# Two attention blocks in one kernel: four score banks per head group on VectorE, processed in pairs, and PV grouped by head

## Chip, cores and metric

The kernel runs on one core of one Trainium2 chip. The metric is the device time of one execution in microseconds. Of the kernel before there are eight runs, with a median of 482.88 us.

## What is computed

The input of each of two attention blocks, A and B, is 2048 rows of 448 bf16 numbers; their outputs stand side by side in rows of 896. Both have 16 heads of 28.

```python
# A: 16 query heads share one key head and one value head
q = (x @ wq).reshape(B, S, H, Dh).transpose(0, 2, 1, 3)
k = x @ wk
v = x @ wv
scores = einsum("bhqd,bkd->bhqk", q, k) * Dh ** -0.5
o = einsum("bhqk,bkd->bhqd", softmax(scores), v)
a = o.transpose(0, 2, 1, 3).reshape(B, S, H * Dh) @ wo
# B: each position sees 8 keys of its own head, at distances 0, 2, ..., 14
logits = einsum("bhsd,bhswd->bhsw", q, kg) * Dh ** -0.5   # masked where the index is negative
b = einsum("bhsw,bhswd->bhsd", softmax(logits), vg).transpose(0, 2, 1, 3).reshape(B, S, D) @ wo
```

A needs 16 x 2048 x 2048 exponentials. They are most of ScalarE's work.

## The kernel before

**The order of the work.** The program is planned in Python before it is built. Every instruction, or small group of them, is added to a list with its engine, an estimated duration, the tiles that it reads (R) and writes (W), a priority `pr` (lower goes first) and sometimes an earliest time. `Sched.run` then plays a list scheduler: whenever an engine is free, it takes the ready operation of lowest priority number. The resulting order on each engine is fixed in the program, and each engine waits on semaphores where the plan has a dependency. Score matmuls and exponentials of A have priority -50, the first VectorE pass -45, PV -40, the later VectorE passes -0.5, the evictions of B -1; other work has its due time in microseconds.

**Part A.** The queries are taken in 4 stretches of 512 rows (`sc`), the 16 heads in 4 groups of four (`t`), so there are 16 head groups ("quads") in time. In each, a unit is one head `j` against one block `tb` of 128 keys: a score bank of 128 keys by 512 queries in PSUM. There are 16 x 4 = 64 units in a quad and 1024 in all. They are taken in order, head innermost, three and two at a time in turn, into two sets of score banks (banks 0 to 2, and 3 and 4), numbered `n`. For each set (`a_loop`):

- PE makes the scores, either with 32 rows of the array (line 740) or, where the planner wants a denser PE, with 128 rows against a zero-padded key copy (line 738);
- ScalarE takes the exponential of the set in one instruction (line 756) into one of the 7 slots of the ring `expT`;
- PE multiplies four units at a time with the values and sums (`v_aug`, line 770) into bank 5; the four matmuls of a group are for the heads j = 0 to 3 of one key block, each in its own 32 columns of the array.

Some units are not given to ScalarE. `offload` takes the last bank of every third three-bank set (`n` a multiple of 6, 28 to 396, key blocks 1 to 13), 51 in all. `d_exp` computes their exponential on VectorE in five passes over 512 columns: a scaled conversion of the score bank to int32 (line 802, the only one that reads PSUM, so it frees the bank), the exponent bits (line 805), two products with the fraction bits (lines 807 and 809), and their product in bf16 into `dexp` (line 812). The result has a constant factor, which a second set of values in `v_aug` takes out. A PV group that has such a unit reads three slices of `expT` and one of `dexp`.

At the end of a quad VectorE copies bank 5 out (line 825), and the sums, their reciprocals (line 836), the copies on GpSimd (line 838) and the final projection (line 861) follow.

**Part B** runs beside A in 16 blocks of 128 positions, with due times 25 us apart: projections (lines 902 and 918), products of queries and shifted keys on VectorE (line 943), sums on PE (line 952), maximum and difference on VectorE (lines 964 and 966), for two blocks together an exponential on ScalarE (line 977), its sum (line 979), reciprocal (line 981) and normalised factors (line 983), then products with the shifted values (line 996), additions (line 1000), transposing matmuls that also sum (line 1007) and the projection (line 1014).

**Filler.** A planner rule adds matmuls on zeros, whose results are not used, where PE would otherwise have little to do (lines 357, 380 and 735).

**Shared memory.** In the first microseconds the tile `d_i` holds the query weights, which GpSimd and VectorE copy out at line 574, and `d_u` holds the squares of the keys (lines 621 and 627, read at line 629).

## Time and profile before

| | |
|---|---|
| median of 8 runs | 482.88 us (482.83 to 488.87) |
| profiled execution: its time, its span | 482.85 us, 480.9 us |
| busy: PE, VectorE, ScalarE, GpSimd | 452.5, 378.9, 456.9, 40.8 us |
| granted TensorE clock | 1.0 |
| first exponential of A starts, last ends | 12.73, 471.85 us |
| idle of ScalarE before exponentials of A | 8.7 us |

In the profile PE is TensorE's matmuls, PEld its weight loads, DVE VectorE, ACT ScalarE, POOL GpSimd and SP SyncE; L756 is line 756 of the kernel. A group of instructions is given as line, engine, operation, output<-inputs, partitions x elements of both with their types, and the count; then busy time in us, the mean duration in ns, and the engine's idle time just before these instructions with what released it. The mean duration counts the overlap of one instruction with the next, so it can exceed the time from start to start. The 40 slices give each engine's busy share in tenths. The chain is followed back from the last instruction to what released it.

### The profile page before, as it was taken

The numbers are of one execution on the slowest core, as the hardware profiler recorded it, in microseconds if no ns is written. First come the engines' busy times: TensorE is split into PE (matmuls) and PEld (weight loads), VectorE is DVE, ScalarE is ACT, GpSimd is POOL, SyncE is SP. The second block draws the span as 40 slices with busy tenths as digits, with TensorE's granted clock in tenths as the row PEclk, the third lists the DMA queues.
The fourth block names the chain that finished last, engine by engine and source line by source line (L and its number), as shares of the span: only waits on it lengthen the run. The fifth ranks groups of instructions, "written<-read, shape, count | busy, mean of one in ns | idle before, by whom it ended". The sixth has DMA issues, their size and how long they took to land.

```text
span 480.9 us, 8734 instructions
## 1 busy us (share of the span) xinstructions
PE 452.5 (94%) x3630; PEld 177.0 (37%) x3630; DVE 378.9 (79%) x703; ACT 456.9 (95%) x431; POOL 40.8 (8%) x71
## 2 busy tenths in 40 slices
PE   8999999999999999999999999998999999998886
PEld 3433334333343443333343433333344243333333
DVE  3335887998778888888878888888968989888673
ACT  3999999999999999999999998999999999999993
POOL 8742000000000000000000000000000000000000
PEclk9999999999999999999999999999999999999999
DMA  8790201020200220002020330002200320202001
GB/s 162 150 228 13 88 27 60 11 78 13 85 11 30 97 95 12 11 2 86 11 93 4 116 97 11 10 11 79 95 12 1 115 99 17 67 24 96 0 1 57
DMA packets 42071, 27.34 MB, mean 57 GB/s; under 512 B 17090, under 2 KB 41968, under 8 KB 42032
## 3 DMA queue, kind: packets, MB, share of 16 engines
q1 hardware_dynamic: 40080, 25.65, 18.5%
q10 hardware_dynamic: 1776, 0.81, 0.7%
q8 instruction: 28, 0.46, 0.4%
q0 software_dynamic: 176, 0.33, 0.3%
q14 instruction: 11, 0.09, 0.1%
HBM read 17.60 MB, written 5.52 MB: 48 GB/s over the span
## 4 chain that ended last, share of the span: by engine, by line
ACT 63%; PE 34%; DMA 1%; DVE 1%; ACTq 0%; issue 0%; DVEq 0%
ACT expT L756 62%; PE ps L740 7%; PE ps L902 6%; PE ps L770 5%; PE ps L738 4%; PE ps L688 2%; PE ps L918 2%; PE ps L830 1%; PE ps L1014 1%; DMA d_i<-in_A_wq_dram 1%; PE ps L615 1%; PE ps L861 1%; PE ps L1007 1%; PE ps L651 1%; PE ps L702 0%; PE ps L380 0%
## 5 line engine op out<-in xcount | busy, mean ns | idle before, releaser
L756 ACT ACTIVATE expT<-ps 128x1024 bf16<-128x1024 f32 (+1 forms) x410 | 449.7, 1222 | 8.7 <-PE ps L740 3.3
L740 PE MATMUL ps<-qT,kT 32*128 32x512 bf16 x734 | 110.2, 384 | 12.4 <-ACT expT L756 9.7
L770 PE MATMUL ps<-expT,v_aug 128*32 128x512 bf16 x973 | 97.6, 389 | 0.1
L738 PE MATMUL ps<-qT,kz 128*128 128x512 bf16 x290 | 84.1, 382 | 8.8 <-ACT expT L756 6.9
L740 PEld LDWEIGHTS ps<-qT,kT 32*128 32x128 bf16 x734 | 27.1, 91 | 81.3 <-ACT expT L756 58.6
L943 DVE TENSOR_TENSOR stage<-qTB,kTB 112x1024 bf16<-112x1024 bf16 x64 | 44.1, 707 | 4.0 <-PE ps L952 4.0
L770 PEld LDWEIGHTS ps<-expT,v_aug 128*32 128x32 bf16 x973 | 24.1, 93 | 62.7 <-issue 57.9
L802 DVE TENSOR_SCALAR d_i<-ps 128x512 int32<-128x512 f32 x51 | 35.3, 693 | 14.3 <-PE ps L740 13.1
L838 POOL COPY rrep<-rden 128x512 bf16<-128x512 bf16 x15 | 12.7, 846 | 399.4 <-DVE rden L836 399.4
L902 PE MATMUL ps<-xT_B,wqkv 128*112 128x512 bf16 (+1 forms) x128 | 43.2, 405 | 0.2 <-DVE qT L711 0.2
L996 DVE TENSOR_TENSOR prod<-Vsh,a_n 128x896 bf16<-128x896 bf16 x64 | 38.2, 627 | 0.0
L807 DVE SCALAR_TENSOR_TENSOR d_u<-d_i 128x512 f32<-128x512 uint16 x51 | 36.1, 707 | 0.0
L809 DVE SCALAR_TENSOR_TENSOR d_v<-d_i,d_e 128x512 f32<-128x512 uint16 x51 | 35.3, 692 | 0.0
L812 DVE SCALAR_TENSOR_TENSOR dexp<-d_u,d_v 128x512 bf16<-128x512 f32 x51 | 34.9, 684 | 0.0
L738 PEld LDWEIGHTS ps<-qT,kz 128*128 128x128 bf16 x290 | 19.3, 99 | 35.0 <-ACT expT L756 28.3
L952 PEld LDWEIGHTS ps<-ones,stage 112*128 112x128 bf16 x512 | 20.9, 96 | 13.4 <-issue 7.9
L952 PE MATMUL ps<-ones,stage 112*128 112x4 bf16 x512 | 25.2, 167 | 0.2 <-DVE qT L711 0.2
L1007 PE MATMUL ps<-ident,padd 128*112 128x128 bf16 x256 | 25.1, 226 | 0.0
L1007 PEld LDWEIGHTS ps<-ident,padd 128*112 128x112 bf16 x256 | 18.9, 129 | 12.3 <-issue 9.4
L902 PEld LDWEIGHTS ps<-xT_B,wqkv 128*112 128x112 bf16 (+1 forms) x128 | 14.3, 127 | 22.1 <-issue 17.2
L805 DVE TENSOR_SCALAR d_e<-d_i 128x512 int16<-128x512 int16 x51 | 21.6, 424 | 0.2
L830 PEld LDWEIGHTS ps<-sel,PV_sb 128*128 128x128 f32 x128 | 18.9, 190 | 5.5 <-issue 3.9
(109 smaller groups left out, 439.7 us busy)
## 6 DMA issues: line engine op xcount, KB each, us to landing
Vsh<-v_scratch SPq DMA_DIRECT2D x16, 896.0 KB, 4.7
v_scratch<-Vst SPq DMA_DIRECT2D x16, 112.0 KB, 1.7
out_dram<-outB SPq DMA_DIRECT2D x16, 112.0 KB, 1.7
out_dram<-outA SPq DMA_DIRECT2D x14, 112.0 KB, 1.8
wqkv<-in_B_wqkv_dram SPq DMA_DIRECT2D x1, 672.0 KB, 4.8
stage<-in_A_x_dram ACTq DMA_DIRECT2D x1, 448.0 KB, 3.7
wo_B<-in_B_wo_dram SPq DMA_DIRECT2D x4, 98.0 KB
wo<-in_A_wo_dram SPq DMA_DIRECT2D x4, 98.0 KB
```

The lines of the kernel that those rows point to most:

```text
L738: r = e.matmul(g.bank(b0 + i), g.kz[:, j, 128 * tb:128 * tb + 128], g.qT[:, sc % 2, t, :], start=True, stop=True)
L740: r = e.matmul(g.bank(b0 + i), g.kT[32 * j:32 * j + 32, 128 * tb:128 * tb + 128], g.qT[32 * j:32 * j + 32, sc % 2, t, :], start=True, stop ...
L756: x = a("act", t_exp(w), lambda e, b0=b0, w=w, n=n: e.activation(g.expT[:, n % ERING, 0:w], g.ps[:, 512 * b0:512 * b0 + w], ACT.Exp, scale ...
L770: x = e.matmul(g.bank(PVBANK, p0=32 * j, p1=32 * j + 32), g.v_aug[:, w, tb, :], src, start=tb == 0, stop=tb == 15, tile_position=(0, 32 * j))
L802: a("dve", t_dve_ps(512), lambda e: e.tensor_scalar(out=ii, in0=g.bank(bank), scalar1=A2 * F, scalar2=-127 * F, op0=ALU.mult, op1=ALU.max) ...
L807: a("dve", t_dve_1x(512), lambda e: e.scalar_tensor_tensor(out=uu, in0=lo, scalar=EP * F, in1=lo, op0=ALU.add, op1=ALU.mult), R=[("d_i", h ...
L809: a("dve", t_dve_1x(512), lambda e: e.scalar_tensor_tensor(out=vv, in0=lo, scalar=ER * F, in1=ee.bitcast(BF16), op0=ALU.add, op1=ALU.mult) ...
L902: a("pe", t_mm(512), lambda e, u=u, t=t, kt=kt, w=w: e.matmul(g.bank(u.bank, p1=KC), g.wqkv[64 * (kt // 3):, kt, w * D + KC * t:w * D + KC ...
L943: op = a("dve", t_dve_2x(1024), lambda e, t=t, qv=qv, kv=kv: e.tensor_tensor(out=g.prodT[0:KC, t, :, :], in0=qv, in1=kv, op=ALU.mult), R=R ...
L952: r = e.matmul(g.bank(u.bank, 128).rearrange("p (h w) -> p h w", w=WIN)[:, 4 * t:4 * t + 4, w], g.prodT[0:KC, t, w, :], g.ones4[:, :], sta ...
L996: a("dve", t_dve_2x(2 * D), lambda e, qr=qr, Vv=Vv, av=av: e.tensor_tensor(out=g.prod2[:, 2 * qr:2 * qr + 2, :].rearrange("p w (d h) -> p ...
L1007: a("pe", 0.09, lambda e, u=u, t=t, w=w: e.matmul(g.bank(u.bank, 128, 128 * t, p1=KC), g.padd[:, w, KC * t:KC * t + KC], g.ident[:, :], st ...
```

## The change

Four units of each quad but the last go to VectorE, one for each head. They are the last banks of the three-bank sets 0, 2, 5 and 7 of the quad, counting only three-bank sets that lie in it whole; in the first quad sets 4, 6, 7 and 9. That is 60 units. The first pass (line 802) still takes one bank when it comes, but into one half of a 1024-column tile; the four other passes are done once for two units, over 1024 columns. One of the two middle results now overwrites `d_i`.

PV groups are formed by head: as units of ScalarE arrive, each waits in a list of its head, and whenever all four heads have one, the first of each make a group, whatever their key blocks. The four units of VectorE make a group of their own. A quad still has 16 groups; the first in the order of forming starts the sums and the last ends them.

In part B the exponential of line 977 writes its result with the window index ahead of the head index, so that its writes are 64 bytes apart, and the factors of line 983 are read and written in that same order. `padd` is no longer a tile of its own but the first half of `prod2`. The value projections of A in `a_v` may get a filler matmul (352 columns) ahead of the first matmul of each block.

```diff
-OFF_EVERY, OFF_FROM, OFF_TO = 6, 28, 396
-DR = 4
+OFF_AT = {q: (0, 2, 5, 7) for q in range(1, 15)}
+OFF_AT[0] = (4, 6, 7, 9)
+DR = 2
...
-                if o.use is not None and o.use.spare and area(T) < self.WANT:
+                if o.use is not None and o.use.spare and o.alone and area(T) < self.WANT:
...
-        self.dexp = sb([128, DR, 512], BF16, "dexp")
-        self.d_i = sb([128, 2, 512], mybir.dt.int32, "d_i")
-        self.d_e = sb([128, 2, 512], mybir.dt.int16, "d_e")
-        self.d_u = sb([128, 1, 512], FP32, "d_u")
-        self.d_v = sb([128, 1, 512], FP32, "d_v")
+        self.dexp = sb([128, DR, 1024], BF16, "dexp")
+        self.d_i = sb([128, 2, 1024], mybir.dt.int32, "d_i")
+        self.d_e = sb([128, 1024], mybir.dt.int16, "d_e")
+        self.d_u = sb([128, 1024], FP32, "d_u")
...
-        self.padd = sb([128, 4, D], BF16, "padd")
+        self.padd = self.prod2[:, 0:4, :]
...
-        u = Use(f"V{c}", g.LB)
+        u = Use(f"V{c}", g.LB, spare=160)
...
+                o.alone = kt == 0
...
+        quads = {(sc, t): [[] for _ in range(4)] for sc in range(4) for t in range(4)}
+        dunits = []
...
-                where.append((us[i], ("expT", n % ERING), g.expT[:, n % ERING, 512 * i:512 * i + 512], 0))
+                quads[us[i][:2]][us[i][3]].append((us[i], ("expT", n % ERING), g.expT[:, n % ERING, 512 * i:512 * i + 512]))
...
-                where.append((us[na],) + g.d_exp(b0 + na, slot) + (1,))
-            while len(where) >= 4 or (where and pos == NU):
-                grp, where = where[:4], where[4:]
-                sc, t, tb, _ = grp[0][0]
-
-                def pv(e, grp=grp):
-                    for (sc, t, tb, j), _, src, w in grp:
-                        x = e.matmul(g.bank(PVBANK, p0=32 * j, p1=32 * j + 32), g.v_aug[:, w, tb, :], src,
-                                     start=tb == 0, stop=tb == 15, tile_position=(0, 32 * j))
-                    return x
-                o = a("pe", 0.33, pv, R=sorted({y[1] for y in grp}) + [(k, w, tb // 4) for k in ("v_aug", "v_aug1") for w in sorted({y[3] for y in grp})],
-                      W=["pv"] if tb in (0, 15) else [], pr=-40, dense=700)
-                if tb == 0:
-                    quad = [o]
-                elif tb < 15:
-                    o.deps.add(quad[0])
-                    quad.append(o)
-                else:
-                    o.deps.update(quad)
-                if pv_first:
-                    o.claims = [PVBANK]
-                    pv_first = False
-                if tb == 15:
-                    g.a_quad_end(sc, t)
+                dunits.append((us[na],) + g.d_exp(b0 + na, slot))
+                if len(dunits) == 4:
+                    g.pv_group(dunits, 1)
+                    dunits = []
+            for u in us:
+                js = quads[u[:2]]
+                while all(js):
+                    g.pv_group([x.pop(0) for x in js], 0)
+
+    def pv_group(self, grp, w):
+        g, a = self, self.s.add
+        qd = grp[0][0][:2]
+        n = len(g.pvs.setdefault(qd, []))
+        first, last = n == 0, n == 15
+
+        def pv(e):
+            for (_, _, tb, j), _, src in grp:
+                x = e.matmul(g.bank(PVBANK, p0=32 * j, p1=32 * j + 32), g.v_aug[:, w, tb, :], src,
+                             start=first, stop=last, tile_position=(0, 32 * j))
+            return x
+        o = a("pe", 0.33, pv, R=sorted({y[1] for y in grp}) + sorted(
+            {(k, w, y[0][2] // 4) for k in ("v_aug", "v_aug1") for y in grp}), W=["pv"] if first or last else [], pr=-40, dense=700)
+        if len(g.pvs) == 1 and first:
+            o.claims = [PVBANK]
...
+        g.pvs[qd].append(o)
+        if last:
+            g.a_quad_end(*qd)
...
-        return int(n % OFF_EVERY == 0 and OFF_FROM <= n <= OFF_TO and 0 < us[-1][2] < 14)
+        g = self
+        if n % 2 or us[0][:2] != us[-1][:2]:
+            return 0
+        if us[0][:2] != g.quad:
+            g.quad, g.round = us[0][:2], n // 2
+        return int(n // 2 - g.round in OFF_AT.get(4 * us[0][0] + us[0][1], ()))
...
+            a("dve", 0.68, lambda e: e.tensor_scalar(out=ee, in0=hi, scalar1=127.0, scalar2=128.0, op0=ALU.add, op1=ALU.mult),
+              R=di, W=["d_e"], pr=-0.5)
+            a("dve", t_dve_1x(1024), lambda e: e.scalar_tensor_tensor(
+                out=uu, in0=lo, scalar=EP * F, in1=lo, op0=ALU.add, op1=ALU.mult), R=di, W=["d_u"], pr=-0.5)
+            a("dve", t_dve_1x(1024), lambda e: e.scalar_tensor_tensor(
+                out=ii.bitcast(FP32), in0=lo, scalar=ER * F, in1=ee.bitcast(BF16), op0=ALU.add, op1=ALU.mult),
+              R=["d_e"], W=di, pr=-0.5)
+            a("dve", t_dve_1x(1024), lambda e: e.scalar_tensor_tensor(
+                out=out, in0=uu, scalar=EQ * F * F, in1=ii.bitcast(FP32), op0=ALU.add, op1=ALU.mult),
+              R=["d_u"] + di, W=[("dexp", m % DR)], pr=-0.5)
+        return ("dexp", m % DR), out[:, 512 * h:512 * h + 512]
...
+        ew = g.e_t[:, par].rearrange("p b w h -> p b h w")
...
-        a("act", t_act(256), lambda e: e.activation(fl(g.e_t), fl(g.lg2), ACT.Exp, scale=SCALE),
+        a("act", t_act(256), lambda e: e.activation(ew, g.lg2[:, par], ACT.Exp, scale=SCALE),
...
-            a("dve", 0.62, lambda e, b=b: e.tensor_tensor(
-                out=g.a_n[:, par, b].rearrange("p w h -> p h w"), in0=g.e_t[:, par, b],
-                in1=g.rs[:, b, :].unsqueeze(2).to_broadcast([128, H, WIN]), op=ALU.mult),
+            a("dve", 0.32, lambda e, b=b: e.tensor_tensor(
+                out=g.a_n[:, par, b], in0=g.e_t[:, par, b],
+                in1=g.rs[:, b, :].unsqueeze(1).to_broadcast([128, WIN, H]), op=ALU.mult),
...
-              R=[("prod2", hf), ("prod2", hf + 2)], W=[("padd", hf)], pr=pr)
+              R=[("prod2", hf), ("prod2", hf + 2)], W=[("padd", hf), ("prod2", hf)], pr=pr)
```

## The prediction, made before the changed kernel was run

> **What bounds the kernel now.** I read the summary page first, then the groups of instructions by shape, the waits of ScalarE, the table of stages and the timeline around ScalarE's longest pauses. The page's busy shares, 40 slices and chain of waits:
>
> ```profile
> span 480.9 us, 8734 instructions
> ...
> PE 452.5 (94%) x3630; PEld 177.0 (37%) x3630; DVE 378.9 (79%) x703; ACT 456.9 (95%) x431; POOL 40.8 (8%) x71
> ...
> DVE  3335887998778888888878888888968989888673
> ACT  3999999999999999999999998999999999999993
> ...
> PEclk9999999999999999999999999999999999999999
> ...
> ACT 63%; PE 34%; DMA 1%; DVE 1%; ACTq 0%; issue 0%; DVEq 0%
> ACT expT L756 62%; PE ps L740 7%; PE ps L902 6%; PE ps L770 5%; PE ps L738 4%; PE ps L688 2%; PE ps L918 2%; PE ps L830 1%; PE ps L1014 1%; DMA d_i<-in_A_wq_dram 1%; PE ps L615 1%; PE ps L861 1%; PE ps L1007 1%; PE ps L651 1%; PE ps L702 0%; PE ps L380 0%
> ```
>
> ScalarE is busy in nine tenths or more of every slice between head and tail, and the chain that ends last lies on it for 63%, nearly all of that in the exponential of line 756. VectorE stands at 79%, near nine tenths in many slices but only at three in the first 36 us. The granted TensorE clock is full throughout. PE's 94% includes filler matmuls and modelled ends. So the end is set by ScalarE's stream: it starts at 12.73 us, its last exponential ends at 471.85, and 9.05 us of tail follow to 480.9. The profiled execution took 482.85 us, 1.95 more than its span, and the median of the runs is 482.88; I count from 482.85.
>
> The groups by shape (count, then busy us and mean ns, then idle before and its releaser):
>
> ```profile
> L756 ACT ACTIVATE expT<-ps 128x1024 bf16<-128x1024 f32 x255 | 258.6, 1064 | 4.6 <-PE ps L770 3.2 <-PE ps L740 0.8 <-PE ps L738 0.2
> L756 ACT ACTIVATE expT<-ps 128x1536 bf16<-128x1536 f32 x154 | 229.0, 1487 | 4.0 <-PE ps L740 2.5 <-PE ps L738 0.9
> ...
> L807 DVE SCALAR_TENSOR_TENSOR d_u<-d_i 128x512 f32<-128x512 uint16 x51 | 36.1, 707 | 0.0
> L802 DVE TENSOR_SCALAR d_i<-ps 128x512 int32<-128x512 f32 x51 | 35.3, 693 | 14.3 <-PE ps L740 13.1 <-PE ps L738 0.7
> ...
> L805 DVE TENSOR_SCALAR d_e<-d_i 128x512 int16<-128x512 int16 x51 | 21.6, 424 | 0.2
> ...
> L983 DVE TENSOR_TENSOR a_n<-e_t,rs 128x128 bf16<-128x128 f32 x16 | 11.4, 755 | 0.1
> ...
> L849 DVE TENSOR_TENSOR oTn<-PV_sb,ps 128x512 bf16<-128x512 f32 x15 | 10.5, 697 | 1.3 <-PE ps L844 1.1
> ...
> L966 DVE TENSOR_TENSOR lg<-ps,mx 128x128 f32<-128x128 f32 x15 | 4.3, 284 | 0.0
> ...
> L977 ACT ACTIVATE e_t<-lg 128x256 f32<-128x256 f32 x8 | 3.6, 455 | 0.0
> ...
> L579 POOL COPY wvB<-Vsh 128x448 bf16<-128x448 bf16 x3 | 2.9, 977 | 0.3
> ...
> L574 POOL COPY wq<-d_i 128x448 bf16<-128x448 bf16 x3 | 1.7, 561 | 0.2
> ```
>
> Two numbers carry the forecast. An exponential over three banks takes 1487 ns and one over two 1064: a bank costs ScalarE 423 ns. And ScalarE stood idle before exponentials for only 8.7 us in all, 3.2 of it in three pauses that a PV matmul (line 770) ended, the ring of expT having no free slot. The timeline of one of them (start, length, engine, line):
>
> ```profile
> 115.62 6.54 ACT L756 ACTIVATE expT<-ps 128x1024 bf16<-128x1024 f32 x6
> ...
> 121.00 0.68 DVE L812 SCALAR_TENSOR_TENSOR dexp<-d_u,d_v 128x512 bf16<-128x512 f32 x1
> ...
> 122.76 0.39 PE L770 MATMUL ps<-dexp,v_aug 128*32 128x512 bf16 x1
> ...
> 123.20 1.94 ACT L756 ACTIVATE expT<-ps 128x1024 bf16<-128x1024 f32 x2 [1.03 <-PE ps L770]
> ```
>
> ScalarE pauses 1.03 us until the PV group at 122.76 has read its inputs. In that group is a dexp operand, which VectorE finished only at 121.68. The pause of 0.5 us near 184 ends on such a group too; the longest, 1.6 us near 289, ends on a group with no dexp in it.
>
> **The change, part by part.** *Banks moved.* Followed through the numbering of score sets, the new rule takes four banks in each of 15 head groups, 60 against 51 now. So 9 three-bank exponentials become two-bank ones, and the number of exponentials stays: 9 x 0.423 = 3.8 us off the binding stream.
>
> *What such a shortened set costs its neighbours.* From starts in the trace, the floor from one exponential to the next is 0.904 us for two banks and 1.331 for three; a shortened set lies 0.064 us above its floor on average, a full one 0.020. Nine more: 9 x 0.044 = 0.4 us back.
>
> *PV regrouped.* No ScalarE group waits for VectorE any more, so the two pauses that end on dexp groups should go: 1.0 + 0.5, and with the overlap of consecutive exponentials lost at a pause (about 0.2 each), 1.9 us. The third I keep, as its group was all ScalarE's: there PE's written order put a score matmul, itself waiting for ScalarE, ahead of the PV that ScalarE needed. Grouping by head makes some units wait for the next key block, four units or 1.6 of the 7 ring slots, less than the chain of five VectorE passes that the ring holds out now. The bounds are a gain of 3.7 (all three go) and a loss of the same size (the delayed heads fill the ring as often); I take 1.9.
>
> *VectorE's passes.* A bank now costs 693 + 424 + 707 + 692 + 684 = 3200 ns, 163.2 us for 51. Between lines 966 (128 columns, 284 ns) and 849 (512, 697) a column costs 1.076 ns, so a pass over 1024 takes about 1.25 us, and the integer pass 424 + 0.26 (half a column's price each, as its 424 suggests) = 0.69 us. A pair: 2 x 0.693 + 0.69 + 3 x 1.25 = 5.83 us, 30 pairs 174.8: 11.6 us more. Line 983 writes its 16 x 8 factors one bf16 every 32 bytes and takes 755 ns, where line 966 with as many columns takes 284; written in order, 16 x 0.47 = 7.5 us go. The sum of line 979 now reads with a stride, at most another 2 us. VectorE goes from 378.9 to some 385 us, still 81%: it costs nothing itself, as long as the three-bank set is freed in time. That is the cover to watch: in all 51 cases of the trace VectorE begins line 802 at a median of 0.05 us after the set's last score matmul and is done 0.70 us (median) before the next score matmul into that set, which again ends 0.18 before its exponential. So a read may be late by 0.88 us for nothing. A pass of 0.69 begun just before never breaks that; one of 1.25 does by up to 0.37. VectorE would be inside such a pass for 90 x 1.25 = 112 of 481 us, 23%: 60 x 0.23 = 14 reads meet one, in three of ten the rest is over 0.88, mean excess 0.18: 0.7 us as PE sees it, of which I take half, 0.35, since VectorE often stands waiting for PE there (13.1 us before line 802). Bounds: nothing, and 60 x 0.37 = 22.
>
> *Softmax factors of part B.* Line 977, on ScalarE, now writes its 256 float32 values 64 bytes apart, where it wrote in order for 455 ns. No ScalarE row shows such a write. Lower bound: no cost. Upper bound: the price of line 983, (755 - 284)/128 = 3.7 ns for each element, so 0.94 us for each of 8, 7.5 us, all on the binding stream. Between them lies GpSimd's pair: line 579 copies 448 columns that it gathers 56 bytes apart in 977 ns, line 574 as many in order in 561: 0.93 ns for each element, 256 x 0.93 = 0.24 us, 1.9 in all. I take that one: another engine than VectorE, and no two-byte writes to merge, although it is a read.
>
> The Trainium skill speaks against this edit: "SBUF — State Buffer", in its note on 16-byte lines, says that every access that crosses to a new line pays a penalty. The 755 against 284 ns of VectorE's strided write agree; whether ScalarE pays is shown by no run here. It gives no size, so the sum stays as it is.
>
> *Rest, taken at nothing.* padd written over the first half of prod2 makes line 996 of the next block wait for the transposes (line 1007) of this one; before, line 1000 had that wait one step later, and it cost 0.7 us once, on VectorE. Should it grow, part B ends later, but its last add starts at 466.8 and its transposes wait in PE's order until 474, so some 5 us cover it. Up to 16 filler matmuls among the v projections in the first 35 us (320 ns each where line 380 does it, up to 16 x 0.3 = 4.8 us of PE) run at the lowest priority; ScalarE idles only 1.1 us in that stage, and their cost is between nothing and perhaps 2 us. The first banks now go to VectorE near 22 us, when the weights that share d_i have been copied out (GpSimd ends line 574 at 12.2) and VectorE is 42% busy (13.2 of 31.6 us). The tail has no offloaded bank and stays.
>
> Sum: 482.85 - 3.8 + 0.4 - 1.9 + 0.35 + 1.9 = **479.8 us**, 0.6% below. About 0.5%, 2.4 us, is what a measurement of this kernel can tell from no change, so this stands just beyond it.
>
> **The rivals.** *A, everything hidden:* ScalarE's strided write is free and all three pauses go: 479.8 - 1.9 - 1.8 = 476.1. For it: line 977 is a plain activation whose output rate nothing here shows to be the limit. Against: pauses come from a written order, and a new order has its own.
>
> *B, the pauses move:* the head that lacks a bank holds its three partners in the ring, and what VectorE held ScalarE for, the ring does: 479.8 + 1.9 = 481.7. For it: a third of the idle time before exponentials is already the ring's.
>
> *C, slower than before: the strided write on ScalarE.* At line 983's price it is 7.5 instead of 1.9 us: 485.4. It decides from the point where the other terms, 5.0 us, are eaten: 5.0/8 = 0.62 us more for each line 977, 1.08 in place of 0.455 us. For it: same geometry, same memory. Against: four bytes instead of two in each write.
>
> *D, VectorE frees the banks late:* if 20 of 60 reads meet a full pass, 20 x 0.37 = 7.4: 486.8. For it: stages of 25 us busy in 28. Against: the read has priority among what is ready, and the median slack of 0.70.
>
> That the change does less than it says can be left out: the count of 60 follows from its numbering.
>
> **How the numbers follow.** The forecast (478 to 481.5) 0.42, A 0.13, B 0.17, C 0.16, D 0.12. Below 480.4: most of the forecast (0.33), A, a little of B, together 0.50. Above 485.3: half of C and D, 0.20. Between: 0.30. The range: A's 476.1 with 0.6 for hidden late reads below, 475.5; above, C and the nearer part of D, 486.0. Forecast's own range: 478 to 481.5.
>
> **What would show it.** The shapes of line 756: 145 with 1536 columns in place of 154, and the same mean durations. Line 977's mean: 455 (A), about 0.7 us (forecast), 1.08 and more (C). Pauses of ScalarE ended by line 770: one, of none on dexp. Line 802 ending as a releaser of score matmuls: D. Line 983 near 0.28 us and the 1024-column passes near 1.25. I am wrong if the mean of line 756 itself moves, if pauses before it grow past 12 us, or if the clock row falls below full anywhere.

## The result

The changed kernel takes 484.44 us (median of 21 runs), the kernel before 482.76 (median of 62 runs). The ratio is 1.0029, with an interval of 1.0014 to 1.0045: 0.3% slower, where 479.8 us, 0.6% faster, had been forecast. The profiled execution took 483.81 us, 0.96 more than that of before, and I compare these two. All medians and ratios of the experiments are of their fast runs, and of two, `to_q15` and `q_prio`, the one profile is of a slow run, with the clock at half for 34 and 41 us.

The summary page of the changed kernel: span, busy shares, the 40 slices of VectorE, ScalarE and the granted clock, the chain of waits by engine:

```profile
span 481.9 us, 8626 instructions
...
PE 453.6 (94%) x3612; PEld 178.9 (37%) x3612; DVE 391.6 (81%) x628; ACT 455.1 (94%) x431; POOL 47.0 (10%) x71
...
DVE  3478887898898888988898898997898899698373
...
ACT  3995999999999999999999999999999999999994
...
PEclk9998999999999999999999999999999999999999
...
ACT 61%; PE 32%; DVE 2%; POOL 2%; DMA 1%; issue 1%; ACTq 0%; DVEq 0%; POOLq 0%
```

ScalarE's stream is unbroken except in one slice: the fourth, 36 to 48 us, shows 5 tenths, and in the same slice the clock falls to 8 tenths. GpSimd, absent from the chain of before, now holds 2% of it. The groups by shape:

```profile
L760 ACT ACTIVATE expT<-ps 128x1024 bf16<-128x1024 f32 x264 | 264.9, 1051 | 7.0 <-PE ps L742 5.7 <-PE ps L744 1.1
L760 ACT ACTIVATE expT<-ps 128x1536 bf16<-128x1536 f32 x145 | 214.0, 1476 | 4.8 <-PE ps L744 4.0 <-PE ps L742 0.5
...
L826 DVE SCALAR_TENSOR_TENSOR d_u<-d_i 128x1024 f32<-128x1024 uint16 x30 | 37.8, 1260 | 0.9 <-PE ps L630 0.9
...
L637 POOL TENSOR_SCALAR kz<-kT,cols 128x512 bf16<-128x512 bf16 x16 | 14.3, 892 | 6.5 <-DVE kT L633 5.3
...
L997 ACT ACTIVATE e_t<-lg 128x256 f32<-128x256 f32 x8 | 5.2, 650 | 0.0
...
L1003 DVE TENSOR_TENSOR a_n<-e_t,rs 128x128 bf16<-128x128 f32 x16 | 4.6, 307 | 0.1
```

The exponential is line 760 now. There are 145 of three banks, as predicted, at 1476 - 1051 = 425 ns a bank. No PV matmul (now line 784) ends a pause of it any more; those that the profile lists all end with score matmuls (lines 744 and 742), and what line 742 ends, the scores against the padded keys `kz`, has grown from 1.1 (0.2 + 0.9, line 738 before) to 6.2 us (5.7 + 0.5).

Where in time this lies is seen when the distance from each exponential to the next is compared with its floor (0.904 us for two banks, 1.331 for three) and summed. The excess is 23.0 us before and 28.2 after. By the 16 head groups it is 2.5 us before and 6.9 after in the first one, and 20.5 against 21.3 in the other fifteen. The timeline of the changed kernel there, all engines:

```profile
32.94 6.21 POOL L637 TENSOR_SCALAR kz<-kT,cols 128x512 bf16<-128x512 bf16 x4 [4.62 <-DVE kT L633]
...
34.63 0.68 DVE L700 CAST qT<-ps 128x512 bf16<-128x512 f32 x1
...
36.96 1.63 DVE L826 SCALAR_TENSOR_TENSOR d_u<-d_i 128x1024 f32<-128x1024 uint16 x1
...
38.70 1.52 DVE L828 SCALAR_TENSOR_TENSOR d_i<-d_i,d_e 128x1024 f32<-128x1024 uint16 x1
...
39.29 2.29 PE L742 MATMUL ps<-qT,kz 128*128 128x512 bf16 x5 [2.37 <-POOL kz L637]
...
40.34 1.02 ACT L760 ACTIVATE expT<-ps 128x1024 bf16<-128x1024 f32 x1 [1.76 <-PE ps L742]
...
41.60 0.28 DVE L671 TENSOR_TENSOR v_aug<-ps,gcol 128x112 bf16<-128x112 f32 x1 [1.38 <-POOL gcol L665]
...
41.80 1.91 DVE L831 SCALAR_TENSOR_TENSOR dexp<-d_u,d_i 128x1024 bf16<-128x1024 f32 x1
43.62 0.41 DVE L702 TENSOR_TENSOR q_sq<-qT 128x512 bf16<-128x512 bf16 x1
...
44.56 0.74 DVE L713 TENSOR_SCALAR qT<-ps,cols 128x512 bf16<-128x512 f32 x1
...
45.99 1.02 ACT L760 ACTIVATE expT<-ps 128x1024 bf16<-128x1024 f32 x1 [2.92 <-PE ps L742]
```

The same four `kz` copies in the kernel before:

```profile
30.51 3.17 POOL L636 TENSOR_SCALAR kz<-kT,cols 128x512 bf16<-128x512 bf16 x4 [3.46 <-DVE kT L632]
```

Two pauses of ScalarE, 1.76 and 2.92 us. Before the first, PE waits 2.37 us for a `kz` copy: the last four take 6.21 us on GpSimd, where they took 3.17 before the change, and VectorE's passes beside them take 1.5 to 1.6 us in place of 1.23. Before the second, the scores wait for the queries of the next head group (`qT`, line 713). VectorE had their source ready at 35.3 us (34.63 + 0.68, the eviction of line 700), but only squares them (line 702) at 43.62: ahead of that in its queue stand the passes of the new banks and a product (line 671) that waits 1.38 us for a tiny `gcol` of GpSimd.

So there were two candidates for the cause, tangled in each other: the **queue** (passes put ahead of work that A's next scores need) and the **contention** (GpSimd and VectorE slowing each other). Rivals outside both: the new layout of the softmax, the halved clock, the fillers in the value projections, and VectorE being too full in general.

### The profile page after: what moved, and what is told of

Read it like the earlier page. It is cut to its first block, busy times and chain, and to the rows that moved or that the text cites. A ratio compares the mean times of both kernels' runs of the same rounds, so it can differ in the third digit from the quotient of the medians.

```text
span 481.9 us, 8626 instructions
## 1 busy us (share of the span) xinstructions
PE 453.6 (94%) x3612; PEld 178.9 (37%) x3612; DVE 391.6 (81%) x628; ACT 455.1 (94%) x431; POOL 47.0 (10%) x71
## 4 chain that ended last, share of the span: by engine, by line
ACT 61%; PE 32%; DVE 2%; POOL 2%; DMA 1%; issue 1%; ACTq 0%; DVEq 0%; POOLq 0%
ACT expT L760 60%; PE ps L744 7%; PE ps L921 6%; PE ps L784 5%; PE ps L742 4%; PE ps L690 3%; PE ps L937 2%; PE ps L849 2%; POOL kz L637 1%; DMA d_i<-in_A_wq_dram 1%; PE ps L880 1%; ACT e_t L997 1%; PE ps L616 1%; PE ps L1034 1%; PE ps L382 1%
## 5 line engine op out<-in xcount | busy, mean ns | idle before, releaser
L760 ACT ACTIVATE expT<-ps 128x1024 bf16<-128x1024 f32 (+1 forms) x410 | 446.7, 1200 | 11.8 <-PE ps L742 6.1
L742 PE MATMUL ps<-qT,kz 128*128 128x512 bf16 x299 | 86.8, 386 | 11.7 <-ACT expT L760 7.0
L784 PE MATMUL ps<-expT,v_aug 128*32 128x512 bf16 x964 | 95.6, 391 | 0.6 <-ACT expT L760 0.5
L816 DVE TENSOR_SCALAR d_i<-ps 128x512 int32<-128x512 f32 x60 | 41.2, 687 | 12.5 <-PE ps L744 9.2
L826 DVE SCALAR_TENSOR_TENSOR d_u<-d_i 128x1024 f32<-128x1024 uint16 x30 | 37.8, 1260 | 0.9 <-PE ps L630 0.9
L831 DVE SCALAR_TENSOR_TENSOR dexp<-d_u,d_i 128x1024 bf16<-128x1024 f32 x30 | 37.6, 1252 | 0.1
L828 DVE SCALAR_TENSOR_TENSOR d_i<-d_i,d_e 128x1024 f32<-128x1024 uint16 x30 | 36.9, 1230 | 0.1
L742 PEld LDWEIGHTS ps<-qT,kz 128*128 128x128 bf16 x299 | 20.5, 99 | 36.7 <-ACT expT L760 25.4
L1027 PE MATMUL ps<-ident,prod 128*112 128x128 bf16 x256 | 25.0, 226 | 0.0
L1027 PEld LDWEIGHTS ps<-ident,prod 128*112 128x112 bf16 x256 | 18.8, 129 | 11.7 <-issue 9.1
L690 PE MATMUL ps<-xT_A,wq 128*128 128x512 bf16 x64 | 21.6, 385 | 0.0
```

The source lines that it names most:

```text
L742: r = e.matmul(g.bank(b0 + i), g.kz[:, j, 128 * tb:128 * tb + 128], g.qT[:, sc % 2, t, :], start=True, stop=True)
L760: x = a("act", t_exp(w), lambda e, b0=b0, w=w, n=n: e.activation(g.expT[:, n % ERING, 0:w], g.ps[:, 512 * b0:512 * b0 + w], ACT.Exp, scale ...
L784: x = e.matmul(g.bank(PVBANK, p0=32 * j, p1=32 * j + 32), g.v_aug[:, w, tb, :], src, start=first, stop=last, tile_position=(0, 32 * j))
L816: a("dve", t_dve_ps(512), lambda e: e.tensor_scalar(out=ii[:, 512 * h:512 * h + 512], in0=g.bank(bank), scalar1=A2 * F, scalar2=-127 * F, ...
L826: a("dve", t_dve_1x(1024), lambda e: e.scalar_tensor_tensor(out=uu, in0=lo, scalar=EP * F, in1=lo, op0=ALU.add, op1=ALU.mult), R=di, W=["d ...
L831: a("dve", t_dve_1x(1024), lambda e: e.scalar_tensor_tensor(out=out, in0=uu, scalar=EQ * F * F, in1=ii.bitcast(FP32), op0=ALU.add, op1=ALU ...
```

## The experiments

Each edit is made to the changed kernel. Ratios are to the kernel before, run beside each experiment, with their intervals. Every edit makes the planner order the whole program anew: over the edits, the excess of ScalarE outside the first group lies between 18.9 and 22.3 us wherever PV is grouped by head (26.0 in `q_prio`). So the first group's excess is the measure of what happens there, and differences of 1 to 2 us in the whole time have other sources too.

**1. No banks in the first head group (`q0_none`).**

```diff
-OFF_AT[0] = (4, 6, 7, 9)
+OFF_AT[0] = ()
```

> The changed kernel with no bank of the first head group on VectorE (56 instead of 60). Theory 'head': in the changed kernel the passes of VectorE in the first head group run beside GpSimd's copies of the padded keys (kz, line 637) and both get slow; PE then waits 2.4 us for kz, its clock halves for 3.4 us, and ScalarE pauses 1.8 and 2.9 us. Without these passes the last four kz copies take 3.2 us together instead of 6.2, the clock stays at 1.0, the first head group's time above ScalarE's floor falls from 7.0 to about 2.5 us; four more banks on ScalarE cost 4 x 0.42 = 1.7 us: 483.8 - 4.5 + 1.7 = 481.0 us. Rival 'order': the pauses come from the re-planned order and the fillers in the value projections, whatever VectorE does: 483.8 + 1.7 = 485.5, pauses and low clock still there. Rival 'spread': the loss lies in all head groups alike; first group unchanged, about 484 to 485.

480.98 us, 0.9954 (0.9933 to 0.9976). With 56 banks instead of 60 it is 3.5 us faster than the changed kernel: the first group's excess falls from 6.9 to 1.7, `kz` takes 701 ns again, and the clock is full up to the tail. The four banks of the first head group are what turned the gain into a loss; the fillers in the value projections, which this kernel keeps, are not.

**2. These four banks in the last head group (`to_q15`).**

```diff
-OFF_AT[0] = (4, 6, 7, 9)
+OFF_AT[15] = (0, 2, 5, 7)
```

> The four banks of the first head group are given to VectorE in the last head group instead (sets 0, 2, 5 and 7), 60 banks as before. Theory 'head': no contention with GpSimd, which has nothing to do there but one copy; clock 1.0, 483.8 - 4.5 = 479.3 us. Rival 'order': 483 to 485. Rival 'VectorE is full at the end': part B ends later and the tail after the last exponential grows from 8.8 us by 1 to 3 us: 481 to 483.

485.8 us, 1.0052 (1.0027 to 1.0076), 4.8 more than `q0_none`, although four banks should spare ScalarE 4 x 0.425 = 1.7. The tail after the last exponential is 14.9 us, 8.8 in `q0_none`: + 6.1 - 1.7 = 4.4, which accounts for the most of it. The tail is read from the one profile, which has the clock at half from 16.9 to 51.0 us; that it is as long in the other runs is not shown. There VectorE is too late with part B: it is busy for 42.9 of the last 51.5 us before the tail, against 33.3 of 50.2 in `q0_none`. So it has little room for banks at the end, but that is another place and another reason than at the start.

**3. Scores of key blocks 12 to 15 in the first group without `kz` (`no_kz3`).**

```diff
-            o.full = len(us) if len(us) > 1 else 0
+            o.full = len(us) if len(us) > 1 and not 49 <= pos <= 66 else 0
```

> All 60 banks as in the changed kernel, but the score matmuls of the first head group's last quarter (key blocks 12 to 15) never use the padded keys kz, so PE has no wait on GpSimd there. Theory 'head': the last kz copies are still slow (about 6 us for four), but PE does not wait for them: no pause of 1.8 us, no halved clock; the second pause (2.9 us, for the queries of the next group, behind a slow VectorE pass) shrinks to under 1.5 us: 480.5 to 481.5 us. Rival: the second pause has its own cause and stays whole: 482 us. Rival 'order': 483.5 or more.

483.22 us, 1.0005 (0.9969 to 1.004). In the profiled execution (481.89 us) the pause on `kz` is gone and the clock is full, but the pause before the queries has grown to 4.66 us and the group's excess is 6.7, against 6.9. Neither the `kz` wait nor the halved clock is the root there: whatever the first pause doesn't take, the second does. In nine of its twelve runs, 483.06 us and more, the granted clock is 0.996 or less, so for those this is not shown.

**4. The softmax layout of before (`old_et`).**

```diff
-        self.e_t = sb([128, 2, 2, WIN, H], FP32, "e_t")
+        self.e_t = sb([128, 2, 2, H, WIN], FP32, "e_t")
...
-        a("act", t_act(256), lambda e: e.activation(ew, g.lg2[:, par], ACT.Exp, scale=SCALE),
+        a("act", t_act(256), lambda e: e.activation(fl(g.e_t), fl(g.lg2), ACT.Exp, scale=SCALE),
...
-                out=g.a_n[:, par, b], in0=g.e_t[:, par, b],
-                in1=g.rs[:, b, :].unsqueeze(1).to_broadcast([128, WIN, H]), op=ALU.mult),
+                out=g.a_n[:, par, b].rearrange("p w h -> p h w"), in0=g.e_t[:, par, b],
+                in1=g.rs[:, b, :].unsqueeze(2).to_broadcast([128, H, WIN]), op=ALU.mult),
```

> The changed kernel with part B's softmax laid out as before the change: ScalarE writes its exponential in order, VectorE writes the factors one bf16 every 32 bytes. If ScalarE's strided write is a price on the binding stream (650 against 455 ns, 8 times): 1.6 us less, 482.2, with VectorE 7 us busier. If VectorE's load is what spreads the small pauses, the 7 us more cost as much or more: 484 or above. The pauses of the first head group are untouched, unless the new order moves them.

484.78 us, 1.0039 (1.0012 to 1.0066). The softmax exponential takes 418 ns instead of 650. That is 8 x 0.232 = 1.9 us by durations, but the excess of the eight gaps that hold it falls only from 3.5 to 2.5 us, so ScalarE's stream gets 1.0 back. And VectorE has its slow factors again and the tail is 10.6 us instead of 8.8: what ScalarE gains the tail loses. The two pauses in the first group stay (excess 8.0, with the clock at half for 6.8 us in this profile, 3.4 in the changed kernel's).

**5. The last four `kz` copies later (`kz3_late`).** The next three runs split queue from contention.

```diff
-                    op0=ALU.mult, op1=ALU.add), R=["jmask", ("kT", c)], W=[("kz", c)], pr=2 + c) for j in range(4)]
+                    op0=ALU.mult, op1=ALU.add), R=["jmask", ("kT", c)], W=[("kz", c)], pr=2 + c, rel=48.0 if c == 3 else 0.0) for j in range(4)]
```

> All 60 banks as in the changed kernel, but GpSimd's last four copies of padded keys (kz of key blocks 12 to 15) come no earlier than 48 us, so that the second pair of VectorE passes in the first head group does not run beside them. Theory 'contention': VectorE's queue stalls in that group because GpSimd, slowed to half by VectorE's passes, delivers the factors of the value projection (line 665) late and VectorE waits for them (1.4 us) and itself runs slow (passes of 1.5 to 1.9 instead of 1.25 us); without it the queries of the next group are in time, both pauses (1.8 and 2.9 us) go: 483.8 - 4.5 = 479.3, at most 480.5 us. Rival 'load': the 11.6 us of passes that go ahead of the query evictions on VectorE are enough; the second pause stays at 2 to 4 us, the first goes: 481.5 to 482.5.

481.23 us, 0.995 (0.9923 to 0.9977). `kz` takes 698 ns and the first pause is gone, but the second stays with 3.05 us: the square of the queries starts at 42.05. The first group's excess is 5.1.

**6. The queries first (`q_prio`).** On VectorE and PE, the evictions, squares and norms of the queries (lines 700 to 713) get priority -1, ahead of the passes.

```diff
-                  R=[u], W=[("qT", par, t)], use=u, pr=pr if first else -1)
+                  R=[u], W=[("qT", par, t)], use=u, pr=min(pr, -1) if first else -1)
```

(and so in the three other places)

> All 60 banks as in the changed kernel; only the priority on VectorE (and of line 704 on PE) of the first four query evictions and squares is set ahead of the later exponential passes. Theory 'order on VectorE': the second pause comes from the queries of the second head group standing behind passes; it goes, although GpSimd's copies still take about 6 us: 483.8 - 3 = 480.8 with the first pause (1.8 us) left, 479.3 if that goes too. Rival 'contention alone': the passes and copies are still slow side by side and something else is late next, the value factors or the PV group of VectorE's four; pauses of 3 us or more remain: 482.5 or above.

493.63 us, 1.0228 (1.0195 to 1.0261): a miss. The queries overtook the last keys as well (`kT`, line 633, which comes at 45.65 us, behind three evictions of queries and all the passes), without which the first group can't end. ScalarE stood 13.8 us, from 33.4 on; the clock fell later, at 36.5. The timeline of ScalarE in this kernel:

```profile
29.09 4.27 ACT L760 ACTIVATE expT<-ps 128x1024 bf16<-128x1024 f32 x4
47.19 3.28 ACT L760 ACTIVATE expT<-ps 128x1024 bf16<-128x1024 f32 x3 [13.83 <-PE ps L744]
```

It shows how closely the order on VectorE decides this stage, but not what the right order is.

**7. The passes last (`pass_low`).** The first two pairs' passes over 1024 columns get priority 14.5, so they come after keys and queries. GpSimd's work is left as it is.

```diff
-              R=di, W=["d_e"], pr=-0.5)
+              R=di, W=["d_e"], pr=14.5 if m < 2 else -0.5)
```

(and so in the three other passes)

> All 60 banks as in the changed kernel; only the four later passes of the first head group's two pairs get a low priority on VectorE (14.5 instead of -0.5), so that the keys and the queries of the second head group go ahead of the second pair. Theory 'queue': the second pause (2.9 us) is the queries' place behind slow passes in VectorE's queue; it goes, whether or not GpSimd is slow: 480 to 481 us, 479.3 if the first pause (1.8 us, for kz) goes too. Rival 'contention': slow passes only move, the PV group of VectorE's four comes late and holds bank 5 or the ring; pauses of 3 us or more remain: 482 to 484.

480.75 us, 0.9941 (0.9913 to 0.9969). Timeline of this kernel:

```profile
31.90 5.89 POOL L637 TENSOR_SCALAR kz<-kT,cols 128x512 bf16<-128x512 bf16 x4 [3.48 <-DVE kT L633]
...
36.89 7.54 ACT L760 ACTIVATE expT<-ps 128x1024 bf16<-128x1024 f32 x7
...
38.78 0.74 DVE L713 TENSOR_SCALAR qT<-ps,cols 128x512 bf16<-128x512 f32 x1
```

Line 713 comes at 38.78 in place of 44.56 us, and where the changed kernel's ScalarE stood for 4.7 us in two pauses, seven exponentials run without one. The excess of the first group is 2.4. All four banks are kept, and the contention too: the last four `kz` copies still take 5.89 us, and a copy of `wvB` (line 580) 1530 ns. In the whole time 0.95 us of the gain is lost again in the tail (9.74 against 8.79 us).

**8. GpSimd out of the way, the queue as it was (`gp_late`).** The change of run 5, and the copies of `wvB` held back to 46 us.

```diff
-                in_=g.wqv[64 * (kt // 3):, kt, :].rearrange("p (h d) -> p d h", d=DH)), R=[("Vsh", 1)], W=[("wvB", kt)], pr=3)
+                in_=g.wqv[64 * (kt // 3):, kt, :].rearrange("p (h d) -> p d h", d=DH)), R=[("Vsh", 1)], W=[("wvB", kt)], pr=3, rel=46.0)
```

> As the run that holds back the last kz copies, and GpSimd's four copies of B's value weights (line 580) come no earlier than 46 us as well, so that only GpSimd's 0.2 us instructions meet the passes of the first head group. There the passes of 1.74 and 1.87 us beside line 580 go back to 1.22, and the pause of 3.2 us in the first group falls by about 1.2 to 2 us, 480 or less, if 'contention' makes it; it stays at 3 us and the time at 480.3 to 481.4, if the load of passes and their place in the queue make it.

480.01 us, 0.9922 (0.9894 to 0.995), but the pause before the queries remains with 2.62 us, and the first group's excess is 4.6:

```profile
39.68 5.06 POOL L580 COPY wvB<-Vsh 128x448 bf16<-128x448 bf16 x4
...
40.71 1.17 DVE L702 TENSOR_TENSOR q_sq<-qT 128x512 bf16<-128x512 bf16 x1
...
43.63 5.12 ACT L760 ACTIVATE expT<-ps 128x1024 bf16<-128x1024 f32 x5 [2.62 <-PE ps L744]
```

The release times are of the plan; on the chip the `wvB` copies began at 39.68 us, beside the last pass and the square of the queries, which took 1.17 us in place of 0.41. So the passes ran at full speed (1.21 to 1.22 us), but some contention stayed.

By the whole time this run is no slower than `pass_low` (480.01 and 480.75 us): what `pass_low` is ahead in the first group, 2.2 us, it is behind in the other groups (21.7 against 19.8 us of excess) and in the tail (1.1). No run says why these differ.

**9. Both (`pass_low_gp`).**

> 60 banks, the passes of the first head group at low priority on VectorE, and GpSimd's kz copies of key blocks 12 to 15 and copies of line 580 held back as well. If contention matters only through the queue: 480.7 us within 0.4, as with the low priority alone, first group about 2.4 us above the floor. If it has a cost of its own: the first group falls below 2 us and the time to 480 or less.

479.78 us, 0.9923 (0.9892 to 0.9954); the profiled execution, with the clock full, took 478.39. The first group's excess is 2.3, against 2.4 with the queue alone: once the order is mended, moving GpSimd's work gains nothing there. It is moved and not gone: the second pair's passes run beside the `wvB` copies here (up to 1.97 us). What the run gains over `pass_low` lies elsewhere, in the tail (8.79 against 9.74 us) and in small pauses.

**10. The contention by itself (`probe`).** This kernel computes nothing of the reference: it runs GpSimd's `kz` copy (128 x 512) eight times alone and then beside each kind of VectorE pass, and some strided writes.

> No part of the reference is computed; the output is zeros. GpSimd makes 8 copies like those of line 637 in each of six stretches: with VectorE idle, and beside ten VectorE instructions of one kind: the pass that reads PSUM (line 816), the integer pass (824), the product of two strided SBUF reads (826), the product of two float32 SBUF reads (831), a bf16 product. Then each VectorE kind alone, then writes and reads with and without a stride on ScalarE and VectorE. Theory 'shared port': 0.70 us each alone and beside PSUM reads; 1.4 us or more beside the kinds with two SBUF sources or the two-elements-a-cycle form, with VectorE slowed too. Rival 'memory busy': all kinds slow them by the same 10 to 30%. Strided float32 write: ScalarE 0.43 to 0.63 us; a strided bf16 write on ScalarE and VectorE costs more than a strided float32 write if two-byte writes are merged, the same if only the line counts.

Timeline of the probe: eight `kz` copies alone, then beside an integer pass (line 45), then beside a product of two operands (line 48):

```profile
6.27 6.21 POOL L115 TENSOR_SCALAR kz<-src,one 128x512 bf16<-128x512 bf16 x8 [5.83 <-DVE f L73]
...
20.70 8.81 POOL L115 TENSOR_SCALAR kz<-src,one 128x512 bf16<-128x512 bf16 x8 [1.04 <-DVE de L45]
30.09 15.52 DVE L48 SCALAR_TENSOR_TENSOR du<-di 128x1024 f32<-128x1024 uint16 x10
31.49 13.06 POOL L115 TENSOR_SCALAR kz<-src,one 128x512 bf16<-128x512 bf16 x8 [1.97 <-DVE du L48]
```

Eight copies take 6.21 us alone, 8.81 beside the integer pass and 13.06 beside the products. For one: 694, 1005 and 1537 ns. VectorE pays as well: the integer pass 694 alone and 1065 ns beside GpSimd, the product 1226 and 1595. A pass that reads PSUM disturbs neither (694 and 691). The strided writes follow below.

**11. What the layout costs, and a cheaper one (`q0_rd`).** `q0_none` with `e_t` written in order by ScalarE and read with a stride by VectorE, so that `a_n` is still written in order.

```diff
-        a("act", t_act(256), lambda e: e.activation(ew, g.lg2[:, par], ACT.Exp, scale=SCALE),
+        a("act", t_act(256), lambda e: e.activation(fl(g.e_t), fl(g.lg2), ACT.Exp, scale=SCALE),
...
-                out=g.a_n[:, par, b], in0=g.e_t[:, par, b],
+                out=g.a_n[:, par, b], in0=g.e_t[:, par, b].rearrange("p h w -> p w h"),
```

> The version without banks of the first head group (481.0 us), and in part B ScalarE writes its exponential in order again (as before the change), while VectorE reads it with a stride of 32 bytes and writes the factors in order. If a strided read of four bytes costs VectorE little (about 0.3 to 0.45 us in place of 0.307), the 8 x 0.2 us of ScalarE come back whole: 479.3 us. If it costs as the strided write did (0.75 us), VectorE is 7 us busier and the tail grows as it did with the old layout (by 1.8 us): 481 us.

480.2 us, 0.9943 (0.9923 to 0.9962). The groups of this kernel:

```profile
L1002 DVE TENSOR_TENSOR a_n<-e_t,rs 128x128 bf16<-128x128 f32 x16 | 5.5, 377 | 0.1
...
L996 ACT ACTIVATE e_t<-lg 128x256 f32<-128x256 f32 x8 | 3.4, 419 | 0.0
```

The exponential takes 419 ns, as in order, the factors 377, half of the 755 of before, and the tail stays at 8.79 us. Of the 1.7 us that line 996 saves by its durations, the exponentials end 0.8 earlier; the excess of the eight gaps that hold it falls by 1.0, from 3.5 to 2.5 us, as in run 4.

**12. and 13. Pairing and PV order by themselves.** Both start from `q0_none`. `q0_single` makes every pass over 512 columns again, for one bank. `q0_single_order` does so too, and groups PV in the order of units as the kernel before did, with VectorE's units inside the groups.

```diff
-            a("dve", 0.68, lambda e: e.tensor_scalar(out=ee, in0=hi, scalar1=127.0, scalar2=128.0, op0=ALU.add, op1=ALU.mult),
-              R=di, W=["d_e"], pr=-0.5)
+        a("dve", 0.4, lambda e: e.tensor_scalar(out=ee, in0=hi, scalar1=127.0, scalar2=128.0, op0=ALU.add, op1=ALU.mult),
+          R=[di], W=[("d_e", h)], pr=-0.5)
...
```

> The version without banks of the first head group (56 banks, 481.0 us), with every VectorE bank processed alone: passes over 512 columns, as before the change, PV by head. VectorE is 56 x 3.20 - 28 x 5.75 = 18 us busier. If pairs only relieve an engine that is not the bound: 481.0 within 0.7 us. If VectorE's load sets part B's end: the tail grows by 1 to 3 us, 482 to 484.

493.29 us, 1.0189 (1.0142 to 1.0236), but not through the banks: the excess is 21.4 and the last exponential ends at 468.0 us, 2.2 earlier than in `q0_none`. Part B is late, and the tail is 23.0 us. VectorE is busy for 388.5 us, only 9.3 more than in `q0_none`. I had not expected so much from so little.

> As the run with single passes, and PV groups of four consecutive units as before the change, so that ScalarE's units wait in the ring for VectorE's. If the grouping by head removes pauses of ScalarE ended by PV (3.2 us idle, 3.7 with the lost overlap, in the kernel before, of which the prediction counted 1.9): 1.9 to 5 us above the run with single passes, and pauses ended by the PV line come back. Rival 'order noise': within 0.7 us of it.

503.98 us, 1.0425 (1.037 to 1.048). ScalarE's waits in this kernel (us in all, times, the longest):

```profile
ACT expT L760 <- PE ps L780: 26.3, 17, 3.9
```

Line 780 is the PV matmul there; `q0_single` has no such wait, and its exponentials end 25.6 us earlier (468.00 against 493.61). With the same banks on VectorE, the grouping by head is worth these 25.6 us of ScalarE's time; of the whole time it is 10.7 us, since the tail is 8.4 us here and 23.0 in `q0_single`. The comparison is for one-bank passes; that of paired ones wasn't made.

**14. to 16. The best of both.** `q0_rd`'s layout on `pass_low_gp`, on `pass_low` and on `gp_late`.

> As the run before, and part B's exponential written in order with VectorE reading it with a stride (377 ns for line 1002 instead of 307). If ScalarE's strided write adds to the rest: 8 x 0.23 = 1.8 us less on ScalarE, 479 us. If VectorE's load at the end takes it back in the tail: 480 to 480.7.

478.4 us, 0.99 (0.9857 to 0.9942), the fastest of all, 4.4 us below the kernel before, with all 60 banks. The page of the profiled execution (477.78 us):

```profile
span 476.0 us, 8632 instructions
...
ACT  3999999999999999999999999999999999999993
```

The gap in the fourth slice is closed.

> Low priority of the first group's passes and part B's exponential in order, GpSimd as in the changed kernel. Additive terms: 480.75 - 1.8 = 479 us. With the tail taking it back: 480 to 480.7.

479.88 us, 0.9919 (0.9888 to 0.9949); excess of the first group 2.4, tail 9.74.

> GpSimd's copies held back (480.0 us), queue priorities as in the changed kernel, and part B's exponential in order. Additive terms: 480.0 - 1.8 = 478.2 us, the pause of 2.6 us in the first group still there. With the tail taking it back: 479.5 to 480.

479.18 us, 0.99 (0.9863 to 0.9937). Its runs lie at two levels, six at 478.8 to 479.2 us with a granted clock of 0.999 to 1.0, and four at 480.3 with 0.996. The profiled one is of the upper: a pause of 3.14 us and 3.4 us of half clock from 38.6.

## Why the prediction was wrong

The sum, from the two profiled executions; measured by the excess over the floors, so the terms add up:

| term | forecast | measured, us |
|---|---|---|
| banks off ScalarE (9 x 0.427 by the floors) | -3.8 | -3.8 |
| PV pauses | -1.9 | -3.7 |
| gaps between exponentials (shortened sets, late bank reads) | +0.75 | +3.5 |
| softmax exponential, strided write | +1.9 | +1.0 |
| first head group | 0 | +4.4 |
| start and tail | 0 | -0.4 |
| sum | -3.05 | +1.0 |

**The step that failed** stands under "Rest, taken at nothing": "The first banks now go to VectorE near 22 us, ... and VectorE is 42% busy". With the sum it put the first head group at nothing; it cost 4.4 us, more than the whole miss of 4.0. The numbers were right, the inference was not. From 12.7 to 36 us VectorE was idle before for more than half of the time; but the free time lay in waits for PE, GpSimd and ScalarE, while what it had to do, keys, values and queries, was needed at once and stood in a fixed order. The new banks' passes (two pairs, 2 x (0.68 + 3 x 1.25) = 8.9 us without the bank reads) have priority -0.5 there, and the preparation has larger numbers, so that the passes go first. I had read the 42% as cover, and not named what stands behind each pass, although the plan's priorities were known. Runs 1, 7, 8 and 9 show it: without the passes, or with the passes behind, the first group's excess is 1.7 to 2.4 us in place of 6.9; with GpSimd's work moved alone, 4.6. The measured time lies between those of rivals B and C (481.7 and 485.4 us), but it came about in neither's way.

**Contention** took part in it, and I had not thought of it. In the changed kernel it made the passes and the copies longer (892 ns for the mean `kz`, 701 where the first group has no banks). With it removed as far as run 8 did, the first group's excess fell by 2.3, from 6.9 to 4.6; with the queue mended, it no longer mattered there (2.4 and 2.3). What it cost there it cost through the queue: with the queries in time, `kz` copies as slow (5.89 us for the last four in run 7) added nothing more. The Trainium skill has the rule, in "Advanced Engine Details and Errata", GPSIMD Details: GpSimd shares a read and a write interface with VectorE and conflicts with VectorE's instructions in a 2-port mode or with two SBUF inputs. The probe agrees: beside the pass with PSUM input a copy took 694 ns, as alone, and beside the products of two SBUF inputs 1537. Beside the integer pass it took 1005; that this pass, with 1024 columns in 694 ns, is in a 2-port mode is not shown.

**PV regrouped**: right in direction, and too small, by a misreading. I kept the third pause, the longest, because no unit of VectorE was in its group. But the pause ends at 292.29 us, past the window that I had looked at (281 to 291), and the last PV group before it has one:

```profile
291.84 0.39 PE L770 MATMUL ps<-dexp,v_aug 128*32 128x512 bf16 x1
...
292.29 1.02 ACT L756 ACTIVATE expT<-ps 128x1024 bf16<-128x1024 f32 x1 [1.62 <-PE ps L770]
```

So all three pauses ended on such groups, and all three went: 3.7, the upper end given, and rival A was right in this. Run 13 shows what the old order does with this many banks: 26.3 us in 17 pauses. **Rival B**, that the pauses move into the ring, is refuted: no exponential waits for line 784.

**Gaps between exponentials** grew by 3.5 us outside the first group, with the gaps of PV pauses and of the softmax exponential left out, where 0.4 + 0.35 was forecast. 2.8 of it lies in the gaps after the exponentials of banks 3 and 4 (12.2 us before, 15.0 after), 2.3 of this where a shortened set came just before (mean gap 0.089 instead of 0.054 us), and 0.6 after the shortened sets themselves. The 0.4 had little behind it in the trace: without the longest PV pause, which happens to follow one, a shortened set lies 0.028 us above its floor in the kernel before, where 0.064 had been taken. No score matmul is recorded as waiting for line 816, and its read begins at a median of 0.05 us after the last score, with 0.71 to spare (the least 0.27). So **rival D** as I put it, full passes ahead of the bank reads, is refuted, and the cause of these small gaps stays open; no run was made for it.

**The strided write**: 650 instead of 455 ns, +0.195 by duration for each of 8, where 0.24 was taken from GpSimd's strided read. The stream paid less: the excess of a gap that holds this exponential rose from 0.31 to 0.44 us, 1.0 us for all 8 where 1.9 was forecast; its duration overlaps with that of its neighbours. Both are far from the 0.62 from which **rival C** would have decided. For the Trainium skill's rule on 16-byte lines, cited in the prediction, the probe has the answer that was missing: ScalarE pays as well (416 ns in order, 633 at 64 bytes apart).

**VectorE's load**: 391.6 us, 385 forecast. The passes were right (1.23 to 1.26 us, 0.68 for the integer one), the factors nearly (307 ns, 284 forecast). "It costs nothing itself" is not refuted for ScalarE's stream in groups 1 to 15, with the cause of the grown gaps open; but runs 2, 4 and 12 show that part B lives on what VectorE has left, and the tail is where it shows.

Of the signs that I named for being wrong, the clock row below full came; the pauses before exponentials rose from 8.7 to 11.8 us, just short of the 12 of the text, and the means of the exponential moved by about 1% (1064 to 1051 and 1487 to 1476 ns).

## What to carry to other kernels

Cover is a place in a queue, not a share of busy time. Before work is put at nothing on an engine that is "42% busy", list what stands behind it in that engine's order in that stage, who waits for it, and for how long; in the ramp at the start of this kernel, where everything is needed as soon as it is there, the answer was 4.4 us. A work item that is added ahead of a shared dependency should go behind the preparation: here four changed priorities were worth 4.5 us in the first group and 3.7 in the whole time (484.44 to 480.75). And a duration is not what an instruction costs the stream, where instructions overlap: compare the distances from start to start.

## What was not expected of the hardware

- **VectorE and GpSimd slow each other** in the probe beside products of two SBUF inputs (a GpSimd copy 694 to 1537 ns, VectorE's 1226 to 1595) and beside the integer pass (694 to 1005, VectorE's 694 to 1065), not beside the pass that reads PSUM. In `kz3_late` a GpSimd instruction of 0.20 us took 1.23 beside a pass.
- **Strided writes** (probe): ScalarE's 256 float32 416 ns in order, 633 at 64 bytes apart, 0.85 ns an element; 256 bf16 at 32 bytes 1322. VectorE's 128 float32 293 and 372, bf16 293 and 693; its strided float32 read 293 and 368. The two-byte writes, at half the distance, cost the most; the layout of run 11, which reads with a stride, does without them.
- **The clock fell without an idle stretch of 3.4 us.** In the changed kernel it fell to half at 38.8 us, within PE's wait of 2.4 us (36.9 to 39.3), for 3.4 us; in the 3.4 us before that, PE had been busy for 1.52. "TensorE: Matmul & The Clock Gate" of the Trainium skill, under What's actually happening, has half clock come after at least one idle window of about 3.4 us. The length agrees, the idleness doesn't: in `gp_late_rd` the clock fell at 38.6 with PE busy for 2.6 of the 3.4 us before, and in `no_kz3` it stayed full although PE was busy for only 1.1 of the 3.4 us from 37.7. What decides it stays open.
